# A decay attention, a dense layer pair and a routed layer pair on one core: four attention blocks ahead of the dense products instead of five

## The chip, the cores and the metric

One core of a Trainium2 chip runs the whole program in one launch. The metric is the device time of one execution, in microseconds (us). The engines are TensorE (PE), VectorE (DVE), ScalarE (ACT), GpSimd (POOL) and SyncE (SP, which here only issues transfers).

## The reference

Three stages, each on the result of the one before. The first is attention with decay, over 2 x 8 heads and 768 positions in 12 blocks of 64 (the kernel takes 128 at a time):

```
intra = einsum('bhic,bhjc->bhij', qb, kb) * Dmask      # lam ** (i - j) on and below the diagonal, 0 above
out   = einsum('bhij,bhjd->bhid', intra, vb) + einsum('bhid,bhde->bhie', qb * lam_pow, kv_state)
kv_state = lam_block * kv_state + einsum('bhsd,bhse->bhde', kb * rev_pow, vb)
```

The second is `g(x @ w_in) @ w_out` with 1536 rows, 512 columns in and out, 2048 between, and g piecewise: 0 below -1, h above 1, (h + 1)^2 / 4 between. The third sends each row to the one of 8 experts that scores highest and computes `gate * (relu(x @ w1[e]) @ w2[e])`.

## The kernel before, in words

**Blocks and chunks.** The 1536 rows are 12 blocks of 128, `m` = 0 to 11, six for each batch entry (`cb = m % 6`); three chunks of four blocks are the moving operands of the dense products, 512 columns each. Layer 1 and its output layer run over `units`: unit n = 8c + g is eighth g of the weights on chunk c. One unit is 24 products of the first layer (two halves f, four slices k, three products each, since values are split into a high and a low part) and 24 of the output layer, which run one unit later (`m1_l1(n, f)`, `m1_l2(n - 1, j)`).

**One attention block** (`attn_pieces`, L314 to L511) has these parts. `prep` (L329) loads the next block's operands and lets GpSimd scale the keys (`kd`, needed for the state) and the queries (`qd`, needed for the product with the state). `masked` multiplies keys and queries on TensorE into two accumulators and VectorE multiplies them by the decay mask into `am`. `outv` multiplies `am` by the values; `outs` adds the queries times the state and splits the result, ScalarE copying the high part `xh` and VectorE subtracting for the low part `xl`. `state_products` and `state_kept` make the next state. Two layouts exist. Blocks below SWAP multiply the whole 128 x 128 square of keys and queries, in products 64 deep. From SWAP = 6 on, the lower half of the heads is turned to the other half of the partitions, and the 64 x 64 quarter above the diagonal is left out: three quarters of the columns, in products that use 64 x 64 corners of the array. That layout needs turned copies of the tables, made by `turn_tables` on GpSimd (L195) behind block 5's masks, and of the block decays, `lamx`, made by four VectorE copies (L469).

**The order.** TensorE runs in program order. `keep_in_program_order` fixes that order also for other engines where it is named; for the rest a scheduler interleaves, and `issue_after` puts an instruction behind another of the same engine. NSTART = 5 blocks (0 to 4) are done ahead of layer 1 by the loop at L1022, with the conversion of the first weight unit between their parts. Block 5's scores then stand behind unit 0 and its output in unit 1; blocks 6 and 7, and in later chunks four blocks each, are spread over the units by `spread`, whose bounds SPREAD are the same for each chunk.

**The weights.** `w_in` and `w_out` come as 64-bit floats, 1 MB for a unit of each, and are turned into 32 bits on the chip once, in chunk 0 (`convert`, L251): ScalarE makes the low words (L267) and the top words (L272), VectorE ors in the sign (L275) and joins (L278), ScalarE copies the high part (L283) and VectorE subtracts for the low part (L287). The joined weights are kept in memory for the later chunks. The first unit of the output layer (WHOLE) is not split. VectorE thus has six conversions of 128 x 1024 a unit in chunk 0. SyncE issues all loads in program order: START_LOADS first, then two weight loads a unit, and a block's operands with the `prep` of the block before it; a load whose buffer is not yet free holds up all loads behind it.

Of the kernel before, what the change touches and what calls it, by code (L numbers as in the profile page):

```python
# [8 lines left out]
F32 = mybir.dt.float32  # L9
F32R = mybir.dt.float32r  # L10
F16 = mybir.dt.float16
I32 = mybir.dt.int32
# [5 lines left out]
P = 128  # L18
# [17 lines left out]
ROUTE = (6.5, 4.5)  # L36
SPREAD = (0.5, 7.75)

WARM = 11
NSTART = 5  # L40
WARM_LAM = 6

SWAP = 6
START_LOADS = "q1 v0 v1 q2 v2 q3 v3 w10 q4 v4 w11 w20"

# [4 lines left out]
def kernel(  # L50
# [144 lines left out]
    def turn_tables():  # L195


        G.tensor_copy(dmask[LOW, 0:4, LOW], dmask[LOW, 4:8, HIGH])
        G.tensor_copy(dmask[LOW, 4:6, LOW], dmask[HIGH, 4:6, HIGH])
        G.tensor_copy(dmask[LOW, 4:6, HIGH], dmask[HIGH, 6:8, HIGH])  # L200
        G.tensor_copy(dmask[HIGH, 4:6, HIGH], dmask[HIGH, 6:8, LOW])
        G.tensor_copy(revx[:, 0:4], rev[:, 0:4])
        G.tensor_copy(revx[LOW, 4:8], rev[HIGH, 4:8])
        G.tensor_copy(revx[HIGH, 4:8], rev[LOW, 4:8])

# [11 lines left out]
    def load_raw(key, src):  # L217
        t = sb.tile([P, 1024], F32, name=f"rw{key[0]}", tag=f"rw{key[0]}")
        SP.dma_start(out=t, in_=src)
        raw[key] = t  # L220

    def load_w(k, n):
# [27 lines left out]

    def convert(key, g):  # L251
# [12 lines left out]
        parts[key] = (f, None) if whole else (hi, lo)  # L264

        def low_word():
            return A.activation(  # L267
                u, low.bitcast(U32), AF.Identity, scale=2.0 ** -29 * (1.0 - 2.0 ** -12), bias=down[:, 0:1],
            )

        def top_word():
            return A.activation(z, top.bitcast(F32), AF.Copy, scale=2.0 ** -112)  # L272

        def sign():
            return V.scalar_tensor_tensor(u, top, -(2 ** 31), u, op0=ALU.bitwise_and, op1=ALU.bitwise_or)  # L275

        def joined():
            return V.scalar_tensor_tensor(  # L278
                f.bitcast(I32), z.bitcast(I32), 3, u, op0=ALU.logical_shift_left, op1=ALU.bitwise_or,
            )  # L280

        def high():
            whi[key] = A.activation(hi, f, AF.Copy)  # L283
            return whi[key]

        def rest():
            wlo[key] = V.tensor_tensor(lo, f, hi.bitcast(F32), op=ALU.subtract)  # L287
            return wlo[key]

        def kept():  # L290
            A.dma_start(out=wsc[key[0], g], in_=f)

        return [low_word, top_word, sign, joined] + ([] if whole else [high, rest]) + [kept]

    def prep_w(k, n):
        if n >= len(units):
            return
        lay, c, g = units[n]
        if lay == 1 and c == 0:
            for f in convert((k, n), g):  # L300
                f()
        else:
            hilo((k, n), raw.pop((k, n)), V)
# [20 lines left out]
    def attn_pieces(m):  # L324
# [4 lines left out]
        def prep():  # L329
            if m >= NSTART - 1 and m + 1 < NBLK:  # L330
                load_attn(m + 1)
# [6 lines left out]

            if cb < 5 and m != NSTART - 1:
                keys()  # L340
            if cb > 0:
# [8 lines left out]
                ast[m, "qd"] = qd  # L350
            if m == NSTART - 1:
                keys()

        def scores():
            prep()
            masked()

        def masked():
# [27 lines left out]
            for h2 in range(2):  # L386
# [7 lines left out]
                ast[m, "A", h2] = am  # L394
            if m == SWAP - 1:
                turn_tables()

# [35 lines left out]

        def outs(between=None):
            pts, banks = ast.pop((m, "o"))
# [10 lines left out]
            for pt, prs in banks:  # L446
                ast[m, "xh"] = kept_order(A.activation(xh[c][:, prs, sl], pt, AF.Copy))
                if between:
                    between()
# [40 lines left out]
        def state_kept():  # L490
# [4 lines left out]
            if cb == 0:  # L495
                kept_order(A.activation(sn, pt, AF.Copy))
            elif m < NSTART:
                kept_order(V.tensor_tensor(sn, pt, ast.pop((m, "decayed")), op=ALU.add))
            else:
# [10 lines left out]
        pieces[m] = (prep, masked, outv, outs)  # L510
        return [scores, None, outp, None] if m >= NSTART else [scores, None, None, st]  # L511


# [502 lines left out]
    for m in range(2):  # L1016
        pieces[m][0]()
    steps = convert((1, 0), 0)
    low_word, top_word, sign, joined, high, rest = [
        lambda f=f: tc.keep_in_program_order(f()) for f in steps[:-1]  # L1020
    ]
# [110 lines left out]
    for n in range(NU):  # L1132
        lay, c, g = units[n]
        if lay == 1 and g == 0:
            if c + 1 < len(CHUNKS):
                m0 = first_blk[c + 1]
                fs = [f for m in range(max(m0, NSTART), m0 + CHUNKS[c + 1]) for f in pcs[m]]
                spread(fs, n + SPREAD[0], n + SPREAD[1])
            if c == 1:
# [219 lines left out]
```

## Time and profile before

| what | value |
|---|---|
| median of 3 runs | 467.77 us (467.75 to 470.25) |
| the profiled execution | 467.34 us, span 465.5 us |
| TensorE busy | 456.6 us, 98% |
| VectorE, ScalarE, GpSimd busy | 327.2, 270.9, 88.9 us |
| mean granted clock | 0.998 |

The span runs from the first to the last instruction; the time of the execution has some 2 us more around it. A busy time is the sum of an engine's instructions; those of TensorE overlap at their ends, so that the distance between two starts tells more than a duration. In the rows of a timeline the first number is the start, the second the time that the merged instructions cover.

### The profile page before, as it was taken

To read this page: it belongs to the slowest core of one execution; us is meant where nothing else is said; L and a number is where in the kernel's file an instruction comes from. 1 tells how busy PE (TensorE), PEld (TensorE's weight loads), DVE (VectorE), ACT (ScalarE), POOL (GpSimd) and SP (SyncE) were. 2 spreads that over 40 slices of the span, in tenths; PEclk is the share of its full clock that TensorE was granted. 3 is DMA by queue.
4 is the path that set the end of the run, shared out by engine and by line. 5 is a ranking of instruction groups with operands and counts; after the bars stand their busy time and mean duration, and the time that the engine had idled before them with its cause. 6 is when DMAs were issued, how large, how long until landed. Compare 5 with 4: busy or idle time off the path is not lost.

```text
span 465.5 us, 7897 instructions
## 1 busy us (share of the span) xinstructions
PE 456.6 (98%) x2947; PEld 375.8 (81%) x2947; DVE 327.2 (70%) x720; ACT 270.9 (58%) x429; POOL 88.9 (19%) x98
## 2 busy tenths in 40 slices
PE   8999999999999999999999999999999999999994
PEld 5875888888888878878888888887778989989993
DVE  6799999997399998574799875576785354453530
ACT  2688887896874554544765655557423543443531
POOL 4521514102004140000000005200045410410202
PEclk9999999999999999999999999999999999999999
DMA  8999979988563342932523325231176443552401
GB/s 333 415 389 375 342 304 363 297 297 258 201 211 112 132 136 92 333 124 87 182 73 128 116 88 180 95 135 48 58 245 219 158 158 119 158 199 77 172 1 53
DMA packets 26880, 86.86 MB, mean 187 GB/s; under 512 B 3986, under 2 KB 7058, under 8 KB 24788
## 3 DMA queue, kind: packets, MB, share of 16 engines
q1 hardware_dynamic: 20066, 68.18, 42.7%
q10 hardware_dynamic: 4322, 11.55, 6.4%
q0 software_dynamic: 2448, 6.56, 4.1%
q8 instruction: 25, 0.41, 0.4%
q14 instruction: 19, 0.16, 0.1%
HBM read 68.44 MB, written 17.90 MB: 185 GB/s over the span
## 4 chain that ended last, share of the span: by engine, by line
PE 70%; issue 18%; DMA 5%; POOL 4%; DVE 1%; POOLq 0%; SPq 0%; ACT 0%; ACTq 0%
PE acc L868 9%; PE l L825 9%; PE acc L870 9%; PE acc L869 9%; PE l L828 9%; PE l L827 9%; DMA rw<-in_w_out_dram 3%; POOL out_dram L876 3%; DMA kv_t<-in_kv_dram 2%; PE m L934 2%; PE m L936 2%; PE m L935 2%; PE acc L863 1%; POOL gate L905 1%; PE sc L370 1%
## 5 line engine op out<-in xcount | busy, mean ns | idle before, releaser
L825 PE MATMUL l<-xh,w1h 128*128 128x512 f32 x192 | 75.0, 396 | 0.3 <-DVE gh L847 0.2
L248 DVE TENSOR_TENSOR w2l<-rw,w2h 128x1024 fp32r<-128x1024 f32 x32 | 39.1, 1223 | 50.8 <-ACT w2h L247 50.8
L868 PE MATMUL acc<-w2h,gh 128*128 128x512 f32 x184 | 72.7, 395 | 0.0
L828 PE MATMUL l<-xh,w1l 128*128 128x512 f32 x184 | 71.7, 390 | 0.0
L870 PE MATMUL acc<-w2h,gl 128*128 128x512 f32 x184 | 71.7, 390 | 0.0
L827 PE MATMUL l<-xl,w1h 128*128 128x512 f32 x184 | 71.6, 389 | 0.0
L869 PE MATMUL acc<-w2l,gh 128*128 128x512 f32 x184 | 71.6, 389 | 0.0
L247 ACT ACTIVATE w2h<-rw 128x1024 fp32r<-128x1024 f32 x32 | 33.9, 1059 | 51.8 <-PE m2a L966 31.1
L851 ACT ACTIVATE gh<-g_t 128x512 fp32r<-128x512 f32 x46 | 28.8, 629 | 36.0 <-DVE g_t L847 36.0
L574 DVE CUSTOM_DVE_ANT_0 jk<-x2s,enb 128x512 f32<-128x512 f32 x72 | 48.2, 699 | 0.9 <-ACT x2s L559 0.6
L248 DVE TENSOR_TENSOR w1l<-rw,w1h 128x1024 fp32r<-128x1024 f32 x32 | 39.7, 1241 | 9.8 <-ACT w1h L247 9.0
L844 ACT ACTIVATE r_t<-l,half 128x512 f32<-128x512 f32 x48 | 32.5, 678 | 23.1 <-PE l L828 22.7
L934 PE MATMUL m<-x2h,w1h 128*128 128x384 f32 (+2 forms) x128 | 43.9, 343 | 0.0
L936 PE MATMUL m<-x2h,w1l 128*128 128x384 f32 (+2 forms) x128 | 43.3, 338 | 0.0
L935 PE MATMUL m<-x2l,w1h 128*128 128x384 f32 (+2 forms) x128 | 43.1, 337 | 0.0
L825 PEld LDWEIGHTS l<-xh,w1h 128*128 128x128 f32 x192 | 35.9, 188 | 8.9 <-DVE gh L847 0.6
L847 DVE SCALAR_TENSOR_TENSOR g_t<-r_t,l 128x512 f32<-128x512 f32 x46 | 31.2, 680 | 16.5 <-ACT r_t L845 16.4
L868 PEld LDWEIGHTS acc<-w2h,gh 128*128 128x128 f32 x184 | 34.5, 188 | 7.5 <-issue 0.5
L870 PEld LDWEIGHTS acc<-w2h,gl 128*128 128x128 f32 x184 | 34.5, 188 | 7.3
L828 PEld LDWEIGHTS l<-xh,w1l 128*128 128x128 f32 x184 | 34.5, 188 | 7.4
L827 PEld LDWEIGHTS l<-xl,w1h 128*128 128x128 f32 x184 | 34.6, 188 | 6.9
L869 PEld LDWEIGHTS acc<-w2l,gh 128*128 128x128 f32 x184 | 34.5, 188 | 6.9
(279 smaller groups left out, 864.6 us busy)
## 6 DMA issues: line engine op xcount, KB each, us to landing
rw<-wsc SPq DMA_DIRECT2D x32, 512.0 KB, 3.3
rw<-in_w_dram SPq DMA_DIRECT2D x32, 512.0 KB, 3.4
rw<-in_w_in_dram SPq DMA_DIRECT2D x8, 1024.0 KB, 9.8
rw<-in_w_out_dram SPq DMA_DIRECT2D x8, 1024.0 KB, 10.6
wsc<-cw ACTq DMA_DIRECT2D x15, 512.0 KB, 7.0
qk_t<-in_qk_dram SPq DMA_DIRECT2D x12, 512.0 KB, 7.4
kv_t<-in_kv_dram SPq DMA_DIRECT2D x6, 512.0 KB, 7.6
x2d<-x2s ACTq DMA_DIRECT2D x12, 256.0 KB, 2.2
```

What stands on the lines that cost most here:

```text
L247: whi[key] = A.activation(hi, r, AF.Copy)
L248: wlo[key] = eng.tensor_tensor(lo, r, hi.bitcast(F32), op=ALU.subtract)
L574: V.tensor_tensor_reduce(out=jk, in0=x2s, in1=enb[e // 2][:, e % 2, :], scale=1.0, scalar=0.0, op0=ALU.mult, op1=ALU.add, accum_out=lr[:, ...
L825: PE.matmul(pt, lhsT=hi[:, f, k, :], rhs=xh[c][:, k, :], start=(k == 0), stop=False)
L827: PE.matmul(pt, lhsT=hi[:, f, k, :], rhs=xl[c][:, k, :], start=False, stop=False)
L828: PE.matmul(pt, lhsT=lo[:, f, k, :], rhs=xh[c][:, k, :], start=False, stop=(k == 3))
L868: PE.matmul(a, lhsT=gh[:, f, sl], rhs=hi[:, f, :], start=(g == 0 and f == 0), stop=False)
L869: PE.matmul(a, lhsT=gh[:, f, sl], rhs=lo[:, f, :], start=False, stop=False)
L870: PE.matmul(a, lhsT=gl[:, f, sl], rhs=hi[:, f, :], start=False, stop=(g == 7 and f == 1))
L934: PE.matmul(pt, lhsT=hi[:, f, k, :], rhs=self.xh[:, k, :], start=(k == 0), stop=False)
L935: PE.matmul(pt, lhsT=hi[:, f, k, :], rhs=self.xl[:, k, :], start=False, stop=False)
L936: PE.matmul(pt, lhsT=lo[:, f, k, :], rhs=self.xh[:, k, :], start=False, stop=(k == 3))
```

## The change

NSTART goes from 5 to 4 and SWAP from 6 to NSTART, so that blocks 4 and 5 are turned too and come among the dense products: in chunk 0 the four blocks 4 to 7 are spread from unit 1.0 to 8.0. The turned tables and decays are made on GpSimd behind block 3's masks, and block 3's state is turned by four GpSimd copies behind `state_kept`. The scaling of block 2's state for block 3 goes from four ScalarE instructions to one of GpSimd. The conversion of the first weight unit is cut in two halves of 512 columns, whose six steps each stand in a fixed order between block 2's scores and the end of block 3; block 3's state is kept behind them. The loads of block 4 come behind those of the weight units 1 and of the first output unit; being turned, its values come in three transfers instead of one. Block 5's loads, issued before by block 4's `prep` ahead of layer 1, come with the `prep` of block 4 in unit 1, and that `prep` stands behind the turned state. The new `load_halves` is called by nothing; the entry `h10` of START_LOADS goes through `load_w`, as `w10` did.

```diff
-SPREAD = (0.5, 7.75)
+SPREAD = ((1.0, 8.0), (0.5, 7.75), (0.5, 7.75))
-NSTART = 5
+NSTART = 4
-SWAP = 6
-START_LOADS = "q1 v0 v1 q2 v2 q3 v3 w10 q4 v4 w11 w20"
+SWAP = NSTART
+START_LOADS = "q1 v0 v1 q2 v2 q3 v3 h10 w11 w20 q4 v4"
...
     def turn_tables():
...
+        def moved(out_, in_):
+            tc.keep_in_program_order(G.tensor_copy(out_, in_))
+
+        moved(revx[:, 0:4], rev[:, 0:4])
+        moved(revx[LOW, 4:8], rev[HIGH, 4:8])
+        moved(revx[HIGH, 4:8], rev[LOW, 4:8])
+        moved(dmask[LOW, 0:4, LOW], dmask[LOW, 4:8, HIGH])
...
+        for g2, o in enumerate((HIGH, LOW)):
+            for h2, r in enumerate(HALVES):
+                moved(lamx[o, h2::2], lamc[r, 2 * g2:2 * g2 + 2])
...
-            if m >= NSTART - 1 and m + 1 < NBLK:
+            if m >= NSTART and m + 1 < NBLK:
                 load_attn(m + 1)
...
         def scores():
-            prep()
+            with ExitStack() as hold:
+                if m == NSTART:
+                    hold.enter_context(tc.issue_after(ast["turned"].ins))
+                prep()
             masked()
...
-            if m == SWAP - 1:
-                turn_tables()
...
         def state_products():
-            if m == NSTART:
-                with tc.issue_after(ast[m, "am"].ins):
-                    for g2, o in enumerate((HIGH, LOW)):
-                        for h2, r in enumerate(HALVES):
-                            V.tensor_copy(lamx[o, h2::2], lamc[r, 2 * g2:2 * g2 + 2])
...
                 kept_order(V.tensor_tensor(sn, pt, ast.pop((m, "decayed")), op=ALU.add))
+                if m == NSTART - 1:
+                    turned = sb.tile([P, 4, 64], F32, name="s_turn", tag="sdec")
+                    for g2, o in enumerate((HIGH, LOW)):
+                        for h2, r in enumerate(HALVES):
+                            ast["turned"] = kept_order(
+                                G.tensor_copy(turned[o, h2::2], sn[r, 2 * g2:2 * g2 + 2])
+                            )
+                    sn = turned
...
                 sd = ast[m + 1, "decayed"] = sb.tile([P, 4, 64], F32, name="sd", tag="sdec")
+                if m + 2 == NSTART:
+                    kept_order(G.tensor_tensor(sd, sn, lamc.to_broadcast([P, 4, 64]), op=ALU.mult))
+                    return
...
     for m in range(NSTART):
-        if m:
+        if m == 3:
+            pieces[m][4]()
+        elif m:
             pcs[m][3]()
-        if m == 3:
-            sign()
         pieces[m][2]()
         if 0 < m < NSTART - 1:
             pcs[m + 1][0]()
         if m == 2:
-            low_word()
-        if m == 4:
-            high()
-            rest()
-        pieces[m][3](joined if m == 3 else None)
-        if m == 2:
-            top_word()
+            turn_tables()
+            low_a()
+            sign_a()
+            top_a()
+        if m == 3:
+            high_a()
+            low_b()
+            sign_b()
+            top_b()
+            joined_b()
+        pieces[m][3]((joined_a,) if m == 2 else ())
         if not m:
             pcs[m][3]()
-        if m == 4:
-            steps[-1]()
+    rest_a()
+    high_b()
+    rest_b()
+    kept()
+    pieces[3][5]()
     at_tags.clear()
```

## Rows read from the trace of the kernel before

**Rows 1.** The page's first part: busy time, share, instructions.

```profile
PE 456.6 (98%) x2947; PEld 375.8 (81%) x2947; DVE 327.2 (70%) x720; ACT 270.9 (58%) x429; POOL 88.9 (19%) x98
```

**Rows 2.** Windows: stretch, its length, then each engine's busy time, clock, DMA share.

```profile
6.30:25.50 19.20, 18.86 (x313) 15.80 (x312) 14.51 (x24) 10.90 (x26) 10.58 (x12) 1.00 1.02 416
...
45.40:56.00 10.60, 10.60 (x71) 8.77 (x71) 10.36 (x11) 8.77 (x13) 4.55 (x3) 1.00 0.97 365
```

**Rows 3.** Timeline of TensorE, 0 to 50 us: start, us, line, operands, count.

```profile
19.35 1.64 PE L364 MATMUL sc<-qk_t 64*128 64x128 f32 x16
20.92 1.09 PE L441 MATMUL ao<-qd,s_new 64*64 64x128 f32 x16
...
25.57 1.19 PE L825 MATMUL l<-xh,w1h 128*128 128x512 f32 x4
...
31.23 1.16 PE L364 MATMUL sc<-qk_t 64*128 64x128 f32 x16
32.33 1.19 PE L825 MATMUL l<-xh,w1h 128*128 128x512 f32 x4
```

**Rows 4.** The chain of waits in order of time: start, us, what.

```profile
38.57 6.87 PE acc L863 x16
45.43 1.03 PE ao L422 x16
46.46 1.02 PE ao L441 x16
...
88.57 0.83 PE sc L370 x32
...
103.22 0.62 PE ao L488 x16
103.84 0.47 PE ao L422 x16
104.31 0.39 PE ao L429 x16
104.70 0.44 PE ao L441 x16
```

**Rows 5.** Timeline of GpSimd: whole and narrow queries, a table turned.

```profile
14.73 1.28 POOL L344 TENSOR_TENSOR qd<-qk_t,wq 128x512 f32<-128x512 f32 x1
...
33.96 0.39 POOL L198 COPY dmask<-dmask 64x256 f32<-64x256 f32 x1 [6.03 <-DVE am L391]
...
51.34 5.86 POOL L349 TENSOR_TENSOR qd<-qk_t,wq 64x256 f32<-64x256 f32 x4 [11.25 <-DMA qk_t<-in_qk_dram]
...
105.33 3.60 POOL L349 TENSOR_TENSOR qd<-qk_t,wq 64x256 f32<-64x256 f32 x4 [19.04 <-DMA wsc<-cw]
```

**Rows 6.** Timeline of VectorE, 0 to 60 us.

```profile
15.61 0.41 DVE L498 TENSOR_TENSOR s_new<-as,sd 128x256 f32<-128x256 f32 x1
16.94 1.29 DVE L391 TENSOR_TENSOR am<-sc,dmask 128x512 f32<-128x512 f32 x2 [0.91 <-PE sc L364]
...
20.03 2.07 DVE L275 SCALAR_TENSOR_TENSOR cu<-rw,cu 128x1024 int32<-128x1024 int32 x1
...
33.93 0.80 DVE L469 COPY lamx<-lamc 64x2 f32<-64x2 f32 x4
...
36.69 1.22 DVE L278 SCALAR_TENSOR_TENSOR w2f<-cz,cu 128x1024 int32<-128x1024 int32 x1
...
42.82 1.21 DVE L287 TENSOR_TENSOR w1l<-cw,w1h 128x1024 fp32r<-128x1024 f32 x1
```

**Rows 7.** Transfer issued at 4.6 us: line, queue, count, KB, us from issue to landing.

```profile
rw<-in_w_in_dram SPq DMA_DIRECT2D x1, 1024.0 KB, 12.7
```

**Rows 8.** Timeline of SyncE's queue: the issue of that transfer.

```profile
4.64 0.56 SPq L240 DMA_DIRECT2D rw<-in_w_in_dram  x1
```

**Rows 9.** Timeline of ScalarE, 0 to 60 us: unit 1's low words and high part.

```profile
26.00 1.24 ACT L267 ACTIVATE cu<-rw,down 128x1024 int32<-128x1024 uint32 x1
...
30.38 1.06 ACT L283 ACTIVATE w1h<-cw 128x1024 fp32r<-128x1024 f32 x1 [0.40 <-DVE cw L278]
```

More of the change, by code (lines that the diff above doesn't have):

```diff
@@ L195, in turn_tables @@
     def turn_tables():
[L198 to L204, printed above, removed]
+        def moved(out_, in_):
[4 more added lines that the diff above has]
+        moved(dmask[LOW, 0:4, LOW], dmask[LOW, 4:8, HIGH])
+        moved(dmask[LOW, 4:6, LOW], dmask[HIGH, 4:6, HIGH])
+        moved(dmask[LOW, 4:6, HIGH], dmask[HIGH, 6:8, HIGH])
+        moved(dmask[HIGH, 4:6, HIGH], dmask[HIGH, 6:8, LOW])
+        for g2, o in enumerate((HIGH, LOW)):
+            for h2, r in enumerate(HALVES):
+                moved(lamx[o, h2::2], lamc[r, 2 * g2:2 * g2 + 2])
     units = [(1, c, g) for c in range(len(CHUNKS)) for g in range(8)]
@@ L220, in load_raw, with load_halves @@
         raw[key] = t
+    def load_halves(k, n):
+        t = sb.tile([P, 1024, 2], I32, name=f"rw{k}", tag=f"rw{k}")
+        src = (w_in if k == 1 else w_out)[units[n][2]].bitcast(I32)
+        for i in range(2):
+            SP.dma_start(
+                out=t[:, 512 * i:512 * i + 512].rearrange("p n t -> p (n t)"), in_=src[:, 1024 * i:1024 * i + 1024],
+            )
+        raw[k, n] = t
     def load_w(k, n):
@@ L249, in hilo, with convert @@
         parts[key] = (hi, lo)
-    def convert(key, g):
+    def convert(key, g, n=1):
         w = raw.pop(key)
@@ L264, in convert, with low_word, top_word, sign @@
         parts[key] = (f, None) if whole else (hi, lo)
-        def low_word():
+        def low_word(s):
             return A.activation(
-                u, low.bitcast(U32), AF.Identity, scale=2.0 ** -29 * (1.0 - 2.0 ** -12), bias=down[:, 0:1],
+                u[:, s], low[:, s].bitcast(U32), AF.Identity, scale=2.0 ** -29 * (1.0 - 2.0 ** -12), bias=down[:, 0:1],
             )
[L271 to L277, printed above, removed]
+        def top_word(s):
+            return A.activation(z[:, s], top[:, s].bitcast(F32), AF.Copy, scale=2.0 ** -112)
+        def sign(s):
             return V.scalar_tensor_tensor(
-                f.bitcast(I32), z.bitcast(I32), 3, u, op0=ALU.logical_shift_left, op1=ALU.bitwise_or,
+                u[:, s], top[:, s], -(2 ** 31), u[:, s], op0=ALU.bitwise_and, op1=ALU.bitwise_or,
             )
-        def high():
-            whi[key] = A.activation(hi, f, AF.Copy)
+        def joined(s):
+            return V.scalar_tensor_tensor(
+                f.bitcast(I32)[:, s], z.bitcast(I32)[:, s], 3, u[:, s], op0=ALU.logical_shift_left, op1=ALU.bitwise_or,
+            )
+        def high(s):
+            whi[key] = A.activation(hi[:, s], f[:, s], AF.Copy)
             return whi[key]
-        def rest():
-            wlo[key] = V.tensor_tensor(lo, f, hi.bitcast(F32), op=ALU.subtract)
+        def rest(s):
+            wlo[key] = V.tensor_tensor(lo[:, s], f[:, s], hi.bitcast(F32)[:, s], op=ALU.subtract)
             return wlo[key]
@@ L291, in kept @@
             A.dma_start(out=wsc[key[0], g], in_=f)
-        return [low_word, top_word, sign, joined] + ([] if whole else [high, rest]) + [kept]
+        steps = [low_word, top_word, sign, joined] + ([] if whole else [high, rest])
+        parts_ = [slice(i * 1024 // n, (i + 1) * 1024 // n) for i in range(n)]
+        return [[lambda op=op, s=s: op(s) for op in steps] for s in parts_], kept
     def prep_w(k, n):
@@ L299, in prep_w @@
         if lay == 1 and c == 0:
-            for f in convert((k, n), g):
+            steps, kept = convert((k, n), g)
+            for f in steps[0]:
                 f()
+            kept()
         else:
@@ L336, in keys @@
                 ast[m, "kd"] = kd
-            if cb < 5 and m != NSTART - 1:
+            if cb < 5:
                 keys()
@@ L432, in outv, with outs @@
                     )
-        def outs(between=None):
+        def outs(between=()):
             pts, banks = ast.pop((m, "o"))
@@ L447, in outs @@
                 ast[m, "xh"] = kept_order(A.activation(xh[c][:, prs, sl], pt, AF.Copy))
-                if between:
-                    between()
+                for f in between:
+                    f()
                 ast[m, "xl"] = kept_order(
@@ L498, in state_kept @@
                 kept_order(V.tensor_tensor(sn, pt, ast.pop((m, "decayed")), op=ALU.add))
+                if m == NSTART - 1:
[4 more added lines that the diff above has]
+                                G.tensor_copy(turned[o, h2::2], sn[r, 2 * g2:2 * g2 + 2])
+                            )
+                    sn = turned
             else:
@@ L1017 @@
         pieces[m][0]()
-    steps = convert((1, 0), 0)
-    low_word, top_word, sign, joined, high, rest = [
-        lambda f=f: tc.keep_in_program_order(f()) for f in steps[:-1]
+    steps, kept = convert((1, 0), 0, 2)
+    (low_a, top_a, sign_a, joined_a, high_a, rest_a), (low_b, top_b, sign_b, joined_b, high_b, rest_b) = [
+        [lambda f=f: tc.keep_in_program_order(f()) for f in fs] for fs in steps
     ]
     for m in range(NSTART):
-        if m:
+        if m == 3:
+            pieces[m][4]()
+        elif m:
             pcs[m][3]()
-        if m == 3:
-            sign()
         pieces[m][2]()
@@ L1137 @@
                 fs = [f for m in range(max(m0, NSTART), m0 + CHUNKS[c + 1]) for f in pcs[m]]
-                spread(fs, n + SPREAD[0], n + SPREAD[1])
+                spread(fs, n + SPREAD[c][0], n + SPREAD[c][1])
             if c == 1:
```

5 lines of the change are left out of this document (2 added, 3 removed).

## The prediction

> **What bounds the kernel now.** I read the totals first: TensorE is busy for 98% of the span and no other engine for more than 70% [rows 1]. The windows say the same stage by stage: in the stretch before the dense products TensorE is busy 18.86 of 19.20 us, among the dense products 10.60 of 10.60, with the clock at its full level; VectorE stands at 14.51 and 10.36 us in the same two windows [rows 2]. So the end is set by TensorE's queue, which is written out by hand. A TensorE instruction that goes is a gain; one that is only moved is none; and VectorE, at 98% in the dense stage, is the engine that can turn a gain into a wait. I therefore compare two things: when the second unit of layer 1 can start, and what attention work TensorE still owes after that.
>
> The sum is made against the profiled execution, 467.34 us (span 465.5). The median of the runs shown, 467.77, is 0.43 above it; the predicted time is for that median.
>
> **TensorE's work.** Before, block 4 is done whole ahead of layer 1, block 5's scores stand between units 0 and 1 (31.23 to 32.33), and unit 1 starts at 32.33 [rows 3]. What is owed after that start is block 5's output: 1.03 + 1.02 = 2.05 us [rows 4]. After, both blocks come later in the turned form. A turned block, from the chain of waits, costs 0.83 for its scores, 0.62 for the state, 0.47 + 0.39 for the values and 0.44 for the product with the state: 2.75 us; block 5 has no state, so 2.13 [rows 4]. Owed after unit 1's start: 4.88 us, 2.83 more than now. **The change gains only by what unit 1 starts earlier than 32.33 - 2.83 = 29.50.**
>
> **When the first product can start.** Block 4's scores stand at 19.35 and block 3's product with the state at 20.92 [rows 3]. With block 4 gone that product moves up to 19.35, if its scaled queries are there. These come from GpSimd at 14.73 + 1.28 now [rows 5]. In the new order GpSimd first scales the state of block 2, which VectorE ends at 15.61 + 0.41 = 16.02 [rows 6]; that scaling is new on GpSimd (it replaces four ScalarE instructions; I take half of 1.28, as it is half as wide, 0.65), then come the keys (about 1.0, between the half and the whole of 1.28) and the queries, 1.28: 19.0. In time, by a third of a us. TensorE is through with block 3 at 20.4.
>
> The first weights are then late next. They land at 4.64 + 12.7 = 17.3 [rows 7, 8], and this does not move: the load keeps its place in SyncE's queue behind the same loads, and it stays one transfer, since the new function that loads halves has no caller. The conversion order is fixed. Halves I take as half of a whole instruction plus a tenth of a us: VectorE 0.68 for half of 1.22 [rows 6]; ScalarE 0.7 and 0.6 for half of 1.24 and 1.06 [rows 9]. VectorE ends block 3's masks at 16.94 + 1.29 = 18.23 [rows 6]; sign 18.9, join 19.6. ScalarE then has the high half 20.2, the second half's low words 20.9, its top words 21.5, and only then block 3's copy of its output, 22.1. The first product needs that copy: between 22.2 and, if GpSimd's copies stretch VectorE's instructions as described below, 22.9. I take 22.6, against 25.57 now [rows 3]. TensorE idles about 2 us before it. The second half's conversion and both low parts end by 24.4, ahead of the products that read them. Unit 0 takes 31.23 - 25.57 = 5.66 us [rows 3], so it ends at 28.3.
>
> **Unit 1's weights.** Their loads move up by a transfer of 1 MB (two attention loads of 512 KB each now come after them), so they are no limit. Their conversion runs now from 26.00 to 30.38 + 1.06 = 31.44, 5.4 us [rows 9]. After, ScalarE is free at about 23.0, but VectorE has the rest of the first unit and block 3's state until 25.0; sign and join, 1.22 each [rows 6], and the high half, 1.06: 28.5 at the earliest. With the whole 5.4 us, from 23.0 plus the 2 us that VectorE is late, 30.4. I take 29.0, nearer the lower end, since the two masks and the activation that lie inside the present 5.4 us partly fall behind it. Unit 1 then starts at 29.0: a gain of 29.50 - 29.0 = **0.5 us**, between 1.6 (22.2 + 5.66 = 27.9) and -0.9.
>
> **Edits costed at nothing.** The eleven small GpSimd copies (turned tables and decays; 0.39 us for the widest [rows 5], so some 3 us) run at 19 to 22, with their first reader, block 4's keys, behind them at 25 or later. Four copies of the state, 1 us, end near 26, and are needed at block 4's output, past 44. The decays' four VectorE copies, 0.80 us [rows 6], go. The first output layer's unit: now joined at 36.69 + 1.22 = 37.9 [rows 6] for products from 38.57 [rows 4], 6.7 us after unit 0's end; 28.3 + 6.7 = 35.0, less the masks and decays now ahead of it (1.3 + 0.8), 32.9, while the products would come at 29.0 + 5.66 + 0.83 = 35.5. SyncE has the loads of block 5 behind two weight loads; they are issued when VectorE has taken the signs of unit 1 and of the first output unit, near 32, for scores past 50. A block now comes every 0.875 of a unit, and three quarters of a unit (5.66 us for 24 of its 48 products, so some 8 us) lie between one block's output and the next one's scores, which take over its accumulators; covered as long as VectorE is not more than that behind.
>
> **VectorE's lead, the cover of all this.** Unit 2's low part is now done at 42.82 + 1.21 = 44.03, and TensorE comes to the unit at 46.46 + 1.02 = 47.5 [rows 4, 6]: a lead of 3.4 us. After, TensorE comes there at 29.0 + 5.66 + 0.83 + 6.87 = 42.4. VectorE loses 4.0 us of work ahead of it (low part of unit 0 1.2, block 4's residue 0.7, masks of block 5 1.3, decays 0.8), gains block 4's narrower masks (1.0) and starts 0.5 earlier: 40.5. But block 4's and 5's queries now take four narrow GpSimd instructions, 3.60 to 5.86 us in place of 1.28 [rows 5], and VectorE's sign takes 2.07 beside GpSimd's work against 1.22 elsewhere [rows 6]. That adds 1 to 1.5 us: 42.0. The low part is read from the third product on, 2 x 5.66/24 = 0.5 us into the unit, so the lead shrinks to some 0.9 us but holds. On this the Trainium skill (SBUF — State Buffer, Who interferes with whom) speaks against the change: a VectorE instruction with two inputs in SBUF and a GpSimd instruction that reads it take turns on one shared port pair, the later one fully blocked. The trace agrees that they slow each other; by that rule alone VectorE would lose all of GpSimd's time, which is the second rival. The sum above goes by the stretched row.
>
> **Rivals.**
> - *Forecast (0.62):* gain of 0.5 us, 467.77 - 0.5 = **467.3**, 466.2 to 468.7 by the bounds.
> - *The first weights are no gate (0.14):* VectorE and ScalarE keep up, unit 1 starts at 27.9: 1.6 us gained, 466.2, and down to 465.4 with the 0.34 us that TensorE idles in the first window now [rows 2] and with the 0.43 us between the profiled run and the median. For it: ScalarE is busy only 10.90 of 19.20 us there [rows 2]. Against: its order is fixed.
> - *VectorE becomes the bound of the early dense stage (0.16), slower:* GpSimd's keys and queries for block 4 (1.0 + 3.6) stop VectorE fully. Unit 2's low part ends at 40.5 + 4.6 = 45.1, needed at 42.9: TensorE waits 2.2 us, and, with no lead left, up to the extra 2.3 us for block 5's queries (3.6 - 1.28): 467.3 + 2.2 = 469.5, to 471.8; the middle, 470.6, is this case's time. It decides where VectorE loses more than 2.4 us to GpSimd before unit 2. For it: 98% busy. Against: the stretched instructions lose half a us to 0.85 each.
> - *The clock falls (0.04), slower:* TensorE's 2 us idle ahead of the first product is longer than what a whole window of [rows 2] leaves idle now; if the clock fell from its upper level (2.4 GHz) to its lower (1.2) for unit 0, its 5.66 us would double: 467.3 + 5.7 = 473.0. Against: the granted clock is 1.00 in each window of [rows 2].
> - Something unforeseen (0.04), such as a load blocked in SyncE's queue: either side.
>
> **Numbers.** Range 465.4 to 470.6: the first two cases and the lower half of the third, some 0.84. One per cent is 4.7 us, about what a measurement can tell from no change. Faster than 463.1 has no mechanism (0.02); slower than 472.4 is the clock and the tail of VectorE's case (0.07); the rest 0.91.
>
> **What would show it.** The first layer 1 product at 22.2 to 22.9, unit 1's at 28 to 29.5 waiting for ScalarE's high half; block 4 and 5 at 2.75 and 2.13 us on TensorE; no wait of TensorE for VectorE near unit 2. A unit 1 start past 30.5, or waits of several us in the dense stage, would prove me wrong; so would a start before 27.

## The result and the profile after

The changed kernel takes **472.05 us** (median of 8 runs, 470.15 to 474.17) against 467.97 us of the kernel before on the same chip: a ratio of 1.008, 95% interval 1.0062 to 1.0098. It is slower by 4.1 us where 0.5 us of gain was forecast, and outside the range given. The profiled execution took 471.36 us (span 469.6), 4.0 above that of before.

The totals of the kernel after stand against [rows 1]; TensorE has the same work, in a longer span:

```profile
PE 456.4 (97%) x3011; PEld 375.0 (80%) x3011; DVE 328.7 (70%) x724; ACT 270.4 (58%) x426; POOL 104.2 (22%) x113
```

TensorE's waits (engine, line, what it waited for: us in total, times, longest) name what is new. A wait at the very start, alike in every kernel here, is left out:

```profile
PE l L850 <- ACT xh L466: 2.3, 1, 2.3
PE sc L391 <- DVE s_new L523: 1.8, 1, 1.8
...
PE tpq L1142 <- DVE ixr L1137: 0.8, 1, 0.8
```

The first of these was forecast (TensorE idles ahead of the first layer 1 product). The second was not: block 5's scores wait for block 4's new state. The timeline of TensorE shows where both lie (columns as in [rows 3]; L850 to L859 are layer 1, L391 scores, L888 and L893 the output layer, L441, L502 and L460 a block's output and state):

```profile
19.70 1.09 PE L460 MATMUL ao<-qd,s_new 64*64 64x128 f32 x16
23.12 1.53 PE L850 MATMUL l<-xh,w1h 128*128 128x512 f32 x4 [2.33 <-ACT xh L466]
...
30.30 1.09 PE L850 MATMUL l<-xh,w1h 128*128 128x512 f32 x4
33.14 0.90 PE L391 MATMUL sc<-qk_t 64*64 64x128 f32 x32
33.97 0.50 PE L850 MATMUL l<-xh,w1h 128*128 128x512 f32 x1
34.30 0.39 PE L852 MATMUL l<-xl,w1h 128*128 128x512 f32 x1
...
46.39 0.39 PE L853 MATMUL l<-xh,w1l 128*128 128x512 f32 x1
46.71 0.69 PE L502 MATMUL ao<-kv_t,kd 128*64 128x64 f32 x16
...
48.08 0.62 PE L460 MATMUL ao<-qd,s_turn 64*64 64x128 f32 x16
48.84 0.50 PE L850 MATMUL l<-xh,w1h 128*128 128x512 f32 x1
...
57.23 0.43 PE L391 MATMUL sc<-qk_t 64*64 64x128 f32 x2
59.41 0.89 PE L391 MATMUL sc<-qk_t 64*64 64x128 f32 x30 [1.76 <-DVE s_new L523]
```

Unit 0 starts at 23.12 and takes 30.30 - 23.12 = 7.18 us, against 5.66 before [rows 3]. The windows (columns of [rows 2]) say why: the granted clock, 1.00 up to 22, falls to 0.50, the lower of its two levels (1.2 of 2.4 GHz), after the 2.33 us of idling, and is back at 1.00 from about 27 on:

```profile
22.00:24.00 2.00, 0.88 (x3) 0.72 (x4) 1.83 (x3) 1.49 (x4) 1.80 (x5) 0.95 1.08 240
24.00:26.00 2.00, 2.00 (x6) 1.51 (x5) 2.00 (x6) 2.00 (x3) 0.94 (x3) 0.50 0.97 235
26.00:28.00 2.00, 2.00 (x7) 1.58 (x7) 1.90 (x2) 0.66 (x2) 1.96 (x2) 0.70 1.01 361
```

Block 4's output is off TensorE at 48.84, but its state is ready only at 58.43 + 0.84 = 59.27. ScalarE's timeline in between: the two copies of the output (`xh`, 128x256) stand among conversions of weights (`cu`, `cz`, `w1h`, 128x1024):

```profile
49.36 1.23 ACT L281 ACTIVATE cu<-rw,down 128x1024 int32<-128x1024 uint32 x1
50.48 1.06 ACT L299 ACTIVATE w1h<-cw 128x1024 fp32r<-128x1024 f32 x1
51.43 1.14 ACT L286 ACTIVATE cz<-rw 128x1024 f32<-128x1024 f32 x1
...
53.04 0.37 ACT L466 ACTIVATE xh<-ao 128x256 fp32r<-128x256 f32 x1
...
55.89 0.37 ACT L466 ACTIVATE xh<-ao 128x256 fp32r<-128x256 f32 x1
```

and VectorE's, where the low parts of the output (`xl`) and the state follow:

```profile
51.76 1.22 DVE L303 TENSOR_TENSOR w1l<-cw,w1h 128x1024 fp32r<-128x1024 f32 x1
53.14 1.23 DVE L294 SCALAR_TENSOR_TENSOR cw<-cz,cu 128x1024 int32<-128x1024 int32 x1 [0.16 <-ACT r_t L869]
54.28 0.42 DVE L470 TENSOR_TENSOR xl<-ao,xh 128x256 fp32r<-128x256 f32 x1
...
58.09 0.41 DVE L470 TENSOR_TENSOR xl<-ao,xh 128x256 fp32r<-128x256 f32 x1
58.43 0.84 DVE L523 SCALAR_TENSOR_TENSOR s_new<-s_turn,lamx,ao 128x64 f32<-128x64 f32 x4
```

These weights are unit 3's and those of the output unit that runs within it; TensorE comes to unit 3 only past 60.

Where the two kernels meet again, at the first scores of block 8, the loss is almost complete. Of TensorE's timeline before, and then after:

```profile
127.07 0.90 PE L370 MATMUL sc<-qk_t 64*64 64x128 f32 x32
```

```profile
130.69 0.90 PE L391 MATMUL sc<-qk_t 64*64 64x128 f32 x32
```

**The balance of the 4.0 us.** Starts differ between executions (see e2_later), so I count from the point where block 3's values are through: 19.35 before, where block 4's scores begin [rows 3], and 19.70 after, where block 3's product with the state begins: 0.35 of the difference. "Block 3's product" below is this point. From there to unit 1's start it is 12.98 us before [rows 3] and 10.60 after: 2.38 gained. From unit 1's start to block 8's scores it is 94.74 before and 100.39 after: 5.65 lost. 0.35 - 2.38 + 5.65 = 3.62 us; the last 0.4 lies behind that, where routing's wait is 0.8 us after and 0.4 in most of the other profiles here.

### The profile page after: what moved, and what is told of

It is laid out like the page before. It is cut to its first block, busy times and chain, and to the rows that moved or that the text cites. A ratio compares the mean times of both kernels' runs of the same rounds, so it can differ in the third digit from the quotient of the medians.

```text
span 469.6 us, 8052 instructions
## 1 busy us (share of the span) xinstructions
PE 456.4 (97%) x3011; PEld 375.0 (80%) x3011; DVE 328.7 (70%) x724; ACT 270.4 (58%) x426; POOL 104.2 (22%) x113
## 4 chain that ended last, share of the span: by engine, by line
PE 62%; issue 18%; POOL 5%; DVE 0%; POOLq 0%
PE acc L893 9%; PE acc L895 9%; PE acc L894 9%; PE l L850 8%; PE l L853 8%; PE l L852 8%; POOL out_dram L901 3%; PE m L959 1%; PE m L961 1%; PE m L960 1%; PE sc L391 1%; POOL xg L922 1%; POOL gate L930 1%; PE m2a L989 1%; PE m2a L991 1%
## 5 line engine op out<-in xcount | busy, mean ns | idle before, releaser
L850 PE MATMUL l<-xh,w1h 128*128 128x512 f32 x192 | 75.7, 399 | 2.5 <-ACT xh L466 2.3
L262 DVE TENSOR_TENSOR w2l<-rw,w2h 128x1024 fp32r<-128x1024 f32 x32 | 40.4, 1262 | 51.3 <-ACT w2h L261 43.8
L893 PE MATMUL acc<-w2h,gh 128*128 128x512 f32 x184 | 72.9, 396 | 0.0
L369 POOL TENSOR_TENSOR qd<-qk_t,wq 64x256 f32<-64x256 f32 x28 | 33.3, 1190 | 65.8 <-PE ao L460 38.8
L850 PEld LDWEIGHTS l<-xh,w1h 128*128 128x128 f32 x192 | 36.0, 188 | 11.1 <-ACT xh L466 2.6
L877 DVE TENSOR_TENSOR gl<-g_t,gh 128x512 fp32r<-128x512 f32 x46 | 34.9, 759 | 10.1 <-ACT gh L876 9.7
L893 PEld LDWEIGHTS acc<-w2h,gh 128*128 128x128 f32 x184 | 34.5, 188 | 7.6 <-issue 0.3
L261 ACT ACTIVATE w1h<-rw 128x1024 fp32r<-128x1024 f32 x32 | 33.8, 1055 | 11.6 <-PE m L960 4.5
```

What stands on the lines that cost most here:

```text
L261: whi[key] = A.activation(hi, r, AF.Copy)
L262: wlo[key] = eng.tensor_tensor(lo, r, hi.bitcast(F32), op=ALU.subtract)
L850: PE.matmul(pt, lhsT=hi[:, f, k, :], rhs=xh[c][:, k, :], start=(k == 0), stop=False)
L893: PE.matmul(a, lhsT=gh[:, f, sl], rhs=hi[:, f, :], start=(g == 0 and f == 0), stop=False)
```

## The experiments

Three theories stood after the comparison. **A**: the fall of the clock ahead of unit 0 costs the time. **B**: block 4's output and block 5's scores stand too close for the order in which ScalarE and VectorE do their work. **C**: the narrow GpSimd queries of blocks 4 and 5 stretch VectorE through their shared access and make it late. Ratios are against the kernel before on the same chip, with their 95% intervals. Kernels are changes of the kernel after, unless another is named.

**e1_fill: keep TensorE busy ahead of unit 0.** Products of zeros into the warm-up accumulator; they take no part in the computation.

```diff
+    for _ in range(9):
+        PE.matmul(wps, lhsT=wz[:, 0:P], rhs=wz, start=True, stop=True)
     rest_a()
```

> The changed kernel with nine TensorE products of zeros (128x512, about 0.23 us each) put into the 2.3 us that TensorE idles ahead of the first layer 1 product. Theory A, the clock: the idle stretch lets the clock fall to its lower level, and unit 0 takes 7.2 us in place of 5.6. With the fillers the granted clock stays at 1.00 through 22 to 28 us, unit 0 takes 5.6 us, and unit 1 starts 0.9 us earlier (near 29.4 in place of 30.3), where the conversion of its own weights stops it; 471.2 us, and less scatter between runs. Rival: unit 1 is held by its weights' conversion alone (high half done at 30.1 in the changed kernel, whatever the clock), so unit 0 gets shorter but unit 1 starts at 30.1 to 30.3 as before, and the time stays at 472.0.

Measured: 472.97 us, 1.0088 (1.0057 to 1.0119). Unit 0 ran at the full clock and unit 1 began 9.74 us after block 3's product in place of 10.60. But block 5's scores then waited 2.6 us for the state, and the clock fell there instead:

```profile
22.00:24.00 2.00, 1.95 (x8) 1.42 (x9) 2.00 (x4) 1.50 (x2) 1.59 (x4) 1.00 1.04 238
56.00:60.00 4.00, 1.41 (x27) 1.20 (x29) 4.00 (x9) 4.00 (x5) 1.10 (x1) 0.86 0.94 327
60.00:67.00 7.00, 7.00 (x41) 5.71 (x35) 6.91 (x9) 5.37 (x8) 0.00 (x0) 0.84 0.84 291
```

The 0.9 us of theory A is there at unit 1 and gone by unit 3: it is not what makes the kernel slow.

**e2_later: block 5's scores and output a quarter of a unit later.**

```diff
-                spread(fs, n + SPREAD[c][0], n + SPREAD[c][1])
+                if c == 0:
+                    for f, s_ in zip([f for f in fs if f], (1.0, 2.0, 3.0, 3.75, 4.5, 5.5, 6.25, 7.0)):
+                        at(n + s_, f)
+                else:
+                    spread(fs, n + SPREAD[c][0], n + SPREAD[c][1])
```

> The changed kernel with block 5's scores a quarter of a unit later (behind the first half of unit 3 in place of ahead of it) and its output a quarter later too; nothing else moves. Theory B: TensorE's wait of 1.76 us at these scores is for accumulators that VectorE, far behind with the weights, frees late; 2.8 us of products put ahead of the scores cover it: the wait goes, 470.3 us. Rival: VectorE is the bound of the stage, so that the wait turns up elsewhere near unit 3 or at block 5's output: 472.0 us.

Measured: 471.48 us, 1.006 (1.0041 to 1.008). Block 5's scores no longer wait (TensorE of e2_later):

```profile
61.33 0.90 PE L391 MATMUL sc<-qk_t 64*64 64x128 f32 x32
```

The 0.5 us that scores still wait for a state in this trace lie at 175.66, in the last chunk. From block 3's product to block 8's scores it is 108.87 us, against 110.99 after and 107.72 before. The state is as late as ever: output off TensorE at 50.2, state ready at 59.90 + 0.84 = 60.74. The median shows less than the trace. In the profiled execution block 3's product comes at 21.39 in place of 19.70, and the first loads are not the cause: the first scores begin at 6.62 in the kernel after and in e2_later, and differ in what they take (first after, then e2_later):

```profile
6.62 2.09 PE L385 MATMUL sc<-qk_t 64*128 64x128 f32 x32
```

```profile
6.62 3.77 PE L385 MATMUL sc<-qk_t 64*128 64x128 f32 x32
```

TensorE's first products run at half their later pace, here until near 10 us and in the kernel after until near 6.7, though the windows give the granted clock as 1.00 there. The runs lie in two groups, 469.8 to 470.2 and 471.3 to 472.3; whether this start parts them is not shown.

**e4_narrow: blocks 4 and 5 with whole queries.** One GpSimd instruction in place of four; the queries are then not turned, and the values come out otherwise.

```diff
-                if m < SWAP:
+                if m < 6:
                     kept_order(G.tensor_tensor(qd, qkt[:, 0], wq, op=ALU.mult))
```

> The changed kernel, but GpSimd scales the queries of blocks 4 and 5 in one whole instruction each in place of four narrow turned ones; the queries are then not turned, which leaves that part of the computation wrong. GpSimd's 5.0 and 6.3 us become 1.3 each. Theory C, the shared port: VectorE's instructions between 39 and 46 us (1.76 us each) go back to 1.22, VectorE is 2.5 to 3 us further at block 5's scores and the wait of 1.76 us goes: 470.3 us. Rival: VectorE is late because of its own work and of ScalarE's order; its instructions shorten by less than 1 us in sum, and a wait of 1 us or more stays: 471 to 472 us.

Measured: 568.17 us in all, which is not comparable: the other values send rows into the overflow loop of the routed stage. Up to 62 us the trace can be read against e2_later, which started within 0.02 us of it. First VectorE in e4_narrow, then in e2_later:

```profile
42.97 1.21 DVE L303 TENSOR_TENSOR w1l<-cw,w1h 128x1024 fp32r<-128x1024 f32 x1
...
58.62 0.84 DVE L523 SCALAR_TENSOR_TENSOR s_new<-s_turn,lamx,ao 128x64 f32<-128x64 f32 x4
```

```profile
43.80 1.75 DVE L303 TENSOR_TENSOR w1l<-cw,w1h 128x1024 fp32r<-128x1024 f32 x1
...
59.90 0.84 DVE L523 SCALAR_TENSOR_TENSOR s_new<-s_turn,lamx,ao 128x64 f32<-128x64 f32 x4
```

The stretch is real (1.75 against 1.21 us) and the state comes 1.28 us earlier without it. Most of that is TensorE's own earlier arrival: from the output's end to the state it is still 9.99 us (49.47 to 59.46), against 10.51 in e2_later (50.23 to 60.74). That is a part of theory C, and less than it said; block 5's scores still wait 1.3 us.

**e5_order: block 3's output copies ahead of the second half's conversion.**

```diff
+        pieces[m][3]((joined_a,) if m == 2 else ())
         if m == 3:
             high_a()
+            rest_a()
             low_b()
...
-        pieces[m][3]((joined_a,) if m == 2 else ())
...
-    rest_a()
```

> The changed kernel with block 3's output copied (high part on ScalarE, low part on VectorE) ahead of the second half's low words, sign, top words and join, in place of behind them; the first half's low part follows at once. The first product then comes near 21.5 in place of 23.1, TensorE idles 0.8 us in place of 2.3, and the clock stays up. Theory A: unit 0 takes 5.6 to 6.2 us (its second half may wait some tenths for its own high half at 24.5). Unit 1 is then held by its weights alone: VectorE reaches them no earlier, so it starts at 29.4: a gain of 0.9 us, 471.2 us. Rival: what sets the start is only block 3's copy, and unit 1 follows at 28: 469.8 us.

Measured: 473.98 us, 1.011 (1.0086 to 1.0134). The first product came at 21.85 with the clock at its level, but unit 1 waited 1.5 us for its weights and began 10.63 us after block 3's product, no sooner than in the kernel after; block 5's scores waited 2.6. Here, as in e1_fill, unit 1 starts when its weights are there, and this order makes them 0.9 us later than they are in e1_fill.

**e3_outearly: block 4's output a quarter of a unit earlier, all else alike.** As e2_later with the positions 1.0, **1.75, 2.75, 3.5**, 4.5, 5.5, 6.25, 7.0, which are those of the kernel after but for the second.

> The changed kernel with block 4's output (values, product with the state, state) a quarter of a unit earlier, ahead of unit 2's first half in place of behind it; block 5's scores stay. So far the wait at block 5's scores ends with VectorE's new state of block 4, about 10.4 us after block 4's output, where the prediction allowed 8. Theory B: it is that latency, 2.9 us more of products between the two cover it, ScalarE and VectorE take the copies 2 to 3 us earlier, and the wait is under 0.5 us; 470.6 us. Rival, VectorE is the bound of units 1 to 3 whatever the order: the state is still done near 59 us (TensorE's own start of block 3's last product taken as 19.7), a wait of 1.5 us or more stays, 472 us.

Measured: **468.71 us, 1.0007 (0.9993 to 1.0022)**. The output is off TensorE at 45.07 and the state done at 50.29, 5.2 us later in place of 10.4. The copies now come ahead of unit 3's conversions, and the clock falls before unit 0 as in the kernel after (0.55 from 24 to 26). VectorE, then TensorE of e3_outearly, whose scores of block 5 run without a gap:

```profile
48.16 0.75 DVE L470 TENSOR_TENSOR xl<-ao,xh 128x256 fp32r<-128x256 f32 x2
48.83 0.66 DVE L523 SCALAR_TENSOR_TENSOR s_new<-s_turn,lamx,ao 128x64 f32<-128x64 f32 x3
50.01 0.28 DVE L523 SCALAR_TENSOR_TENSOR s_new<-s_turn,lamx,ao 128x64 f32<-128x64 f32 x1
```

```profile
56.69 0.90 PE L391 MATMUL sc<-qk_t 64*64 64x128 f32 x32
```

Its only wait for a state, 0.3 us, lies at 173.21, in the last chunk. One moved output takes back 3.4 us (0.73% between the ratios), with the fall of the clock left in. Between the two traces, from block 3's product to block 8's scores, it is 2.3 us (108.73 against 110.99).

**e6_late: all blocks later.** As e2_later with the positions 2.0, 2.75, 3.5, 4.25, 5.0, 5.75, 6.5, 7.25.

> The changed kernel with blocks 4 to 7 spread from unit 2.0 to 8.0 in place of 1.0 to 8.0, every part three quarters of a unit behind the one before. Theory B': VectorE has its lead of only 0.4 to 0.9 us at units 1 to 3 and gains it later; the blocks' work put a unit later meets it with more lead. The wait at block 5's scores goes, unit 2's products wait less than 0.3 us for their low part; 470 us. Rival: any place costs the same, VectorE is behind by then too: a wait of 1 us or more at the scores of block 5 or 6, 471.5 us.

Measured: 471.77 us, 1.0068 (1.0049 to 1.0087), not what I expected. Another reader is late in the same way: the second half of unit 2 waits for the activation of unit 1's second half, which on VectorE stands behind a weight conversion and block 4's masks.

```profile
PE l L850 <- DVE g_t L872: 2.4, 1, 2.4
```

```profile
47.12 1.21 DVE L303 TENSOR_TENSOR w2l<-cw,w2h 128x1024 fp32r<-128x1024 f32 x1
48.26 1.01 DVE L412 TENSOR_TENSOR am<-sc,dmask 128x384 f32<-128x384 f32 x2
49.19 0.67 DVE L872 SCALAR_TENSOR_TENSOR g_t<-r_t,l 128x512 f32<-128x512 f32 x1
```

**e7_late_fill: e6_late with the fillers of e1_fill.**

> The same with the nine products of zeros ahead of the first layer 1 product. Theory A on top: no fall of the clock ahead of unit 0 and none behind a wait at block 5's scores, so the granted clock is 1.00 from 20 to 70 us in every profile; 469 us, 0.9 us below the one without fillers. Rival: VectorE and ScalarE give the pace of units 0 to 3, what unit 1 starts earlier it waits later: the same as without fillers.

Measured: 471.48 us, 1.0054 (1.0033 to 1.0075). The wait for the activation is 2.8 us, and the clock fell behind it (0.83 from 50 to 56). What the fillers save at unit 0 is given back there.

**e8_half: the kernel before with block 5 alone turned.** Five blocks stay ahead of layer 1; the state of block 4 is turned by four GpSimd copies.

```diff
-SWAP = 6
+SWAP = 5
...
+                if m == NSTART - 1:
+                    turned = sb.tile([P, 4, 64], F32, name="s_turn", tag="sdec")
+                    for g2, o in enumerate((HIGH, LOW)):
+                        for h2, r in enumerate(HALVES):
+                            G.tensor_copy(turned[o, h2::2], sn[r, 2 * g2:2 * g2 + 2])
+                    sn = turned
```

> The kernel before with one part of the change alone: block 5 turned (three quarters of the columns), the state of block 4 and the tables turned behind block 4; five blocks ahead of layer 1 as before, the first weights converted whole, no other order changed. TensorE has 0.27 us less at block 5's scores and 0.6 us less at its output, less 0.2 us for the change of shape. Theory C' (GpSimd's four narrow queries, 5 to 6 us in place of 1.7, and four state copies stretch VectorE by 1.5 us just where unit 1's weights and the first output unit are converted, with a lead of 0.5 us): TensorE waits 0.5 to 1.5 us there, and the time is 468 to 469. Rival: the stretch is covered, 467.2 us.

Measured: **467.49 us, 0.9978 (0.9961 to 0.9995)**. Four narrow queries among the dense products are there here too, and TensorE waits for none of it, against the theory that they alone are too much. The gain fits the turned form: scores 0.83 us in place of 1.10, output 1.45 in place of 2.05 [rows 3, 4], in sum 0.87; the medians differ by 0.92.

**e9_out_fill: e3_outearly with the fillers of e1_fill.**

> The run with block 4's output a quarter earlier, and with the nine products of zeros ahead of the first layer 1 product. Theory A (the clock): in the run without them unit 0 took 7.0 us at a granted clock of 0.55 to 0.59; now 5.6, no stretch under 1.00 before 450 us, unit 1 starts 9.7 us after the start of block 3's product with the state in place of 10.4, and 0.7 us of the whole goes: 468.0 us. Rival: VectorE gives the pace of units 1 and 2, the 0.7 us comes back as waits for its low parts and accumulators: 468.7 us.

Measured: 468.94 us, 1.0023 (1.0009 to 1.0038); one of its 12 runs took 762 us, at a mean granted clock of 0.558 (0.995 to 0.998 in the others); what lowered it there is open. The clock stays at 1.00 and unit 1 starts 9.71 us after block 3's product, 0.73 sooner than in e3_outearly, but TensorE's waits take it back:

```profile
24.00:26.00 2.00, 2.00 (x10) 1.63 (x10) 2.00 (x5) 2.00 (x3) 0.98 (x2) 1.00 0.94 328
```

```profile
PE l L850 <- DVE g_t L872: 0.5, 1, 0.5
...
PE l L850 <- ACT w1h L299: 0.4, 1, 0.4
```

By the second half of unit 2 it is 28.84 us from block 3's product against 29.06, and the medians show no gain. Up to block 8's scores it is 108.51 us against 108.73. The fall of the clock costs next to nothing in the end; TensorE's waits for ScalarE and VectorE say that these two set the pace of the units.

**e10_early_fill: e9_out_fill with block 4's scores at 0.5.**

> The same, and block 4's scores at the end of unit 0 in place of inside unit 1, where block 5's scores stand in the kernel before. TensorE waits 0.4 us for unit 1's high part there anyway (ScalarE's copy); with 0.83 us of scores in the gap the wait goes: 467.6 us. Rival: the masks then come earlier on VectorE, ahead of the first output unit's conversion, and TensorE waits for that instead: 468.0 us or more.

Measured: 469.34 us, 1.0029 (1.0014 to 1.0044). The wait for unit 1's weights is gone, and block 5's scores do not wait; the 1.1 us that scores wait for a state lie at 175.81, in the last chunk, and layer 1 waits 0.4 us for an activation at 74.62. No better than e3_outearly.

**e11_copies_first: TensorE's order untouched.** Only in unit 2 the conversions are written behind the place of block 4's output.

```diff
-                prep_w(1, n + 1)
-                if n:
+                if n != 2:
+                    prep_w(1, n + 1)
+                if n and n != 2:
                     prep_w(2, n)
...
                 place(n, f)
+                if n == 2 and f == 0:
+                    prep_w(1, n + 1)
+                    prep_w(2, n)
```

> The changed kernel with one thing written in another order: in unit 2, the conversions of unit 3's weights and of the next output unit's come behind block 4's output in the program instead of ahead of it. TensorE's order is the same, product for product; no work is added or taken. Theory B, in its sharper form: the wait at block 5's scores is made by the order in which ScalarE and VectorE take block 4's copies and state, behind six conversions that nobody needs yet. Now the state is done 4 to 6 us after block 4's output in place of 10.4, the wait goes, and with it the clock falls that follow it in some runs: 469.3 us. Rival: VectorE is full, and the order only chooses who waits: unit 3's products or its output unit wait 1.5 us or more for their weights, 472 us.

Measured: **469.55 us, 1.0028 (1.0011 to 1.0045)**. Block 4's output ends at 48.42 and its state at 52.17 + 0.28 = 52.45, 4.0 us later. Block 5's scores run without a gap (the only wait for a state, 0.6 us, lies at 173.58, in the last chunk), and unit 3's low part is still in time (its first reader stands at 58.20). TensorE, then VectorE of e11_copies_first:

```profile
48.42 0.50 PE L850 MATMUL l<-xh,w1h 128*128 128x512 f32 x1 [0.16 <-DVE g_t L872]
...
56.81 0.90 PE L391 MATMUL sc<-qk_t 64*64 64x128 f32 x32
57.64 0.50 PE L850 MATMUL l<-xh,w1h 128*128 128x512 f32 x1
```

```profile
48.71 0.42 DVE L470 TENSOR_TENSOR xl<-ao,xh 128x256 fp32r<-128x256 f32 x1 [0.35 <-ACT xh L466]
...
52.17 0.28 DVE L523 SCALAR_TENSOR_TENSOR s_new<-s_turn,lamx,ao 128x64 f32<-128x64 f32 x1
...
55.23 1.22 DVE L303 TENSOR_TENSOR w1l<-cw,w1h 128x1024 fp32r<-128x1024 f32 x1
```

With the narrow queries, the fall of the clock and VectorE's whole work all left in, 0.5% (2.4 us) comes back by the order alone. That is theory B.

**e12_half_decays: e8_half with the decays turned on GpSimd** (ahead of layer 1, in `turn_tables`) in place of VectorE's four copies [rows 6].

```diff
+        for g2, o in enumerate((HIGH, LOW)):
+            for h2, r in enumerate(HALVES):
+                G.tensor_copy(lamx[o, h2::2], lamc[r, 2 * g2:2 * g2 + 2])
...
-                            V.tensor_copy(lamx[o, h2::2], lamc[r, 2 * g2:2 * g2 + 2])
```

> The kernel before with block 5 alone turned, as run above (467.5 us), and with the four copies of the turned decays on GpSimd ahead of layer 1 in place of VectorE. In that run the four copies took VectorE 1.02 us right ahead of the activation for which unit 1's second half waited 0.3 us. Theory: the 0.3 us go, nothing else changes: 467.2 us. Rival: GpSimd's four copies, 0.4 us each, push its queries and keys back and stretch VectorE elsewhere: 467.5 us or more.

Measured: **467.23 us, 0.9976 (0.996 to 0.9993)**, 0.8 us under the kernel before, and the shortest median of all. Unit 1's second half no longer waits 0.3 us for an activation; the intervals of e8_half and e12_half_decays overlap, so that this last step is not told apart.

## Why the prediction was wrong

**The step that failed** is the sentence that three quarters of a unit, some 8 us, lie between one block's output and the next one's scores, "covered as long as VectorE is not more than that behind". The gap was right (48.84 to 57.2 is 8.4 us). The other side was not worked out: from output to state took 10.4 us. I had looked at how late VectorE is in all, and not at which instructions stand ahead of ScalarE's two copies and VectorE's six small instructions that free the accumulators. Ahead of the first copy were conversions whose readers came 7 us later. (What comes every 0.875 of a unit is a part of a block, scores or output, and not a block.) e3_outearly and e11_copies_first shorten those 10.4 us to 5.2 and 4.0 and take back 3.4 and 2.4 us. A cover has to be checked by the queue of each engine that the chain goes through, in program order.

**The start held.** The first product was forecast at 22.6 (22.2 to 22.9) and came at 23.12, or 22.77 with the 0.35 us taken off by which this execution was late. Unit 1 was forecast at 29.0, 9.65 us after block 3's product, held by its high half. In e1_fill and e9_out_fill, where the clock holds, it is 9.74 and 9.71, and it waits there for that high half. In the kernel after the clock adds 0.9.

**The clock** was a rival with 0.04 and 5.7 us. It fell, and unit 0 took 1.5 us more and not 5.66, as it ran slowly only from some 24 to 27. The windows of before, with no such idle time, could not speak on it. Even the 1.5 us did not count: 0.9 were left at unit 1 and next to nothing at the end (e9_out_fill against e3_outearly). In the kernel after, the wait would have taken their place: in e1_fill, where the clock holds at unit 0, block 5's scores are held up for 58.89 - 55.87 = 3.02 us in place of 59.41 - 57.23 = 2.18.

**VectorE as the bound** was the rival nearest in time (469.5 to 471.8), but not in its place: TensorE waits for no low part at unit 2. The lead of 0.9 us forecast there did go: the low part ends at 42.41 + 1.75 = 44.16, and its first reader stands at 44.22. The reader was late by the start (0.35) and the clock (0.95), the low part by VectorE. In e1_fill and e2_later, where the clock holds, TensorE does wait 0.3 us for this low part: the rival was there, and small. The stretch taken as 1 to 1.5 us is 1.28 in e4_narrow at the state. With the rule of the Trainium skill (SBUF — State Buffer, Who interferes with whom), that such instructions take turns, the trace agrees: beside block 5's four queries four VectorE instructions lost 0.53 to 0.55 us each (at 39.58, 41.26, 42.41 and 44.08), 2.2 us in sum, and the queries took 6.32 us together, where the shortest such query of this trace takes 0.73. So GpSimd's time beside VectorE is itself mostly waiting, and VectorE lost 2.2 of some 4 x 0.73 = 2.9 us. The rival had counted GpSimd's stretched time, 3.6 us, as VectorE's loss.

**What TensorE owes** was too low by 0.64 us. The wait's 1.76 us leave out that two of block 5's scores had begun; all scores are held up from 57.23 to 59.41, 2.18 us. 5.65 - 2.18 = 3.47, against 2.83. Each stay of an attention block among dense products costs time at both its edges, which the chain's durations left out: a product ahead of it takes 46.71 - 46.39 = 0.32 us and one behind it 34.30 - 33.97 = 0.33 where the others take 0.23. That is 0.2 us a stay, and there are four after unit 1's start in place of one: 0.6. Block 4's output adds 0.2 more (48.84 - 46.71 = 2.13 for a forecast of 1.92) and block 5's 0.1 (70.06 - 68.62 = 1.44 for 1.30). Against these, 0.3 us that unit 1's first half lost before are gone: it took 35.51 - 32.33 = 3.18 us up to the second half, which there waits for an activation, and takes 33.14 - 30.30 = 2.84 up to block 4's scores. Without the wait e3_outearly has 98.29 - 94.74 = 3.55 here.

**Costed at nothing, rightly:** no weight load was late, and TensorE waited for no turned table. Wrong in size but harmless: the four copies of the state took 3.27 us and not 1 (a spread over 25.8 to 29.1 beside VectorE's work), with their reader past 48; the eleven copies ahead of them took 5.35 and not 3, with their reader at 29.17.

So from the forecast of -0.5 us: wait +2.18, owed +0.64, unit 1's start +0.95 (by the clock, and else by a longer wait), start of this execution +0.35, behind block 8 +0.4: +4.0. Taking the wait away gets a tie, not a gain: the change moves work and takes none away, but for the turned form of blocks 4 and 5, and block 5's is worth 0.9 us in e8_half without moving anything.

## What to carry to other kernels

When a block of work is moved among other work, follow its result to its next user through every engine's queue, and count what stands ahead there; slack of the engine as a whole does not help an instruction that is written behind work which nobody needs yet. Write the short copies that free an accumulator ahead of long conversions that have time. And ask of each part of such a change whether it takes work off the bound engine: here only the turned form did, and it could be had alone.

## What the runs showed of the hardware

- TensorE's clock fell in some executions after 2.3 us without products ahead of unit 0 (the kernel after, e3_outearly, e11_copies_first: a granted clock of 0.50 to 0.55 from 24 to 26 us) and not in others after as long (e2_later, e4_narrow, e6_late: 2.32, 2.31 and 2.31). The latter three are executions with late first products (last point); whether the two hang together is not shown. It also fell behind waits of 2.6 and 2.8 us (e1_fill, e5_order, e7_late_fill), and not behind the 1.76 us of the kernel after and the 2.43 us of e6_late. The low stretch ahead of unit 0 cost about 1.5 us.
- Turned copies on GpSimd are dear beside VectorE: of the four of 64x128 in the kernel after, two took 1.27 and 1.29 us beside VectorE's conversions, and two 0.28 and 0.29 while VectorE stood idle.
- TensorE's first products run at half their later pace for a time that differs between executions: warm-up products of 128x512 start 0.43 us apart and later 0.22, from some 4.4 us on in e1_fill and from near 10 in e2_later, with a granted clock of 1.00 in the windows of both. This moves block 3's product from 18.60 us (e1_fill) to 21.52 (e10_early_fill), more than the effect of several of these changes; only ratios of many runs told them apart.
